# Query transposes of a linear-attention and GEGLU block: 32x32 block transposes on VectorE in place of TensorE transposes, another order of tokens, and a new order of all work

## The chip, the core and the metric

The kernel runs on one core of a Trainium2 chip. A core has four compute engines that are used here: TensorE (PE, matmuls; its weight loads are listed apart as PEld), VectorE (DVE), ScalarE (ACT) and GpSimd (POOL). A fifth, SyncE (SP), issues all transfers (DMA) between DRAM and the on-chip memory. Matmul results arrive in PSUM, in eight banks of 128 x 512 f32. The metric is the device time of one execution in microseconds (us).

## The reference

The input x has 2048 tokens of 512 channels. With xn the layer norm of x, there are 32 heads of 16 channels:

```python
q, k, v = split(xn @ wqkv)                    # 32 heads x 16
phi = lambda t: where(t > 0, t + 1, exp(t)) + 1e-6
pq, pk = phi(q), phi(k)
kv  = sum over tokens of pk (outer) v         # 16 x 16 per head
z   = sum over tokens of pk
o   = (pq @ kv) / (pq . z + 1e-6)
s   = o.reshape(S, D) @ wo
g   = silu((gelu(x @ w_gate) * (x @ w_up)) @ w_down)    # inner width 1792
out = x + s * g
```

Nothing in it depends on the order of the tokens: keys are summed over all of them, and everything else is done token by token.

## The kernel before

**Precision and products.** Everything is f32. A matmul operand is split into a high part (a cast to the reduced format fp32r) and a low part (the rest), and a product is the sum of three: high by high, low by high, high by low. The helper `sum3` issues them; its matmuls all stand on line 537, 128x128 by 128x512 each. Large products are done in 2x2 blocks with seven block products instead of eight. X, Y, Z and V are the PSUM banks of such a scheme: FX, FY, FZ in the up and gate products of the FFN, DX, DY, DZ in its down product, SX, SY, SZ in the last stage. The sums and differences that the scheme needs are VectorE and GpSimd additions.

**Stages.** First come layer norm, key and query projections, `phi` and the accumulation of keys against tokens (up to about 140 us). The scaled-up queries `qp` go to DRAM (`q_d`), with tokens on the 128 partitions. Then the FFN runs over the second 1024 tokens (p = 1, to about 345 us) and over the first 1024 (p = 0, to about 547 us), 14 steps each, with the weights stored in DRAM in split form between the two. The results `acc` get their silu and are kept, for p = 1 in DRAM (`g1_d`). The last stage multiplies the scaled queries, channels on the partitions, with a 512x512 matrix m (kv times wo, in split form `ms`), multiplies by the gate, adds x and stores the output with channels as rows.

**The queries.** Between the steps of the second FFN half stands `queries(i)`, eight calls, for two tiles of 128 tokens each. The table `PAIRS` says at which step. One call loads two tiles q (256 KB each) from DRAM; GpSimd multiplies them with the key sum (tile u, helper `tt` on line 521); VectorE reduces u over each head (line 1193), adds the small constant (1194), takes the reciprocal (1196) and scales q with it (1199). TensorE then transposes the two tiles with eight 128x128 transposes into two PSUM banks `ptq` (line 1206; the banks come from places 5, 6, 7), and ScalarE copies them into the tile pT (helper on line 515). One store of 512 KB takes pT to `pn_d`, laid out by partition, channel block and token; each piece of it is 256 tokens, 1 KB. At the start of the last stage, `s_forms` loads `pn_d` into tiles pb, 256 KB at a time; their casts and sums are the operands Xh, Xl, sf of the SX, SY, SZ products. `s_quad` then takes the gate v, the product and the row of x through its chain of VectorE and GpSimd operations.

**Memory.** Tiles live in numbered places of the pool `dp`. The queries use places 12 (q), 13 (u) and 14 (pT), one after the other; other stages use the same places before and after. `tile_in` gives a place to a new tile, and the class `Gen` remembers the tile before it, all of whose uses have to be over first.

**The order of the work.** The kernel first records every operation with an assumed duration (class `Plan`, method `do`). TensorE's order is given by a list of keys (`pe_keys`), in which ("QT", i) stands for the transposes of call i. ScalarE, VectorE, GpSimd and the transfers are ordered by a list scheduler with due times, which simulates the engines. From its first order it goes on by a table of random seeds (`STEPS`, then `MORE`): each seed moves the due times of the operations in a small window of time a little and plans again. The four engines then get their instructions in that order. All transfers are in one SyncE queue, in the order in which they become due; an entry in that queue waits until its sources are ready and its target is free, and the entries behind it wait too. There are never more than eight transfers under way: the queue waits for the one that is eight back.

The last lines of a call, as the program has them:

```python
pts = [bank(ring("ptq", [5, 6, 7]), f"ptq{t0 + n}", (P, KT, P)) for n in range(2)]
for n in range(2):
    copy("ACT", pTs[:, :, n * P:(n + 1) * P], pts[n], D, "pqT")
dma(pn_d[...](j // 2, ...), pTs, 512, "pieces")
PAIRS = {2: [0], 3: [1], 4: [2], 5: [], 6: [], 7: [3], 8: [4], 9: [5], 10: [], 11: [6], 12: [7]}
```

Of the kernel before, what the change touches and what calls it, by code (L numbers as in the profile page):

```python
# [47 lines left out]
class Gen:  # L48


    def __init__(self, prev):
        self.prev, self.ops, self.over = prev, set(), False
        if prev:
            prev.over = True

# [24 lines left out]
class Plan:  # L80
# [9 lines left out]
    MARGIN = (0.2, 0.2, 3.0)  # L90
    STEPS = (12, 17, 30, 37, 54, 58, 64, 68, 88, 91, 95, 112, 120, 130, 135, 178, 219, 243, 254, 272, 291, 296, 307, 334, 350, 358, 391, 399, 421, 482, 518, 595, 713, 745, 884, 952, 1037, 1318, 1332, 1383, 1390, 1412, 1459, 1532, 1540, 1563, 1676, 1910, 1984, 2062, 2080, 2109, 2148, 2154, 2161, 2184, 2185, 2285, 2316, 2343, 2539, 2627, 2682, 2732, 2736, 2755, 2779, 2791, 2797, 2850, 2885, 3006, 3525, 3544, 3782, 3810, 3819, 4355, 4555, 4804, 4809, 5047, 5174, 5351)
    MORE = ()
    WAIT = 0.3
# [7 lines left out]
    def do(self, eng, cost, fn, out, *ins, more=(), key=None, name="", kb=0, kind="load"):  # L101
# [32 lines left out]
        for v in (out, *more, *ins):  # L134
            if isinstance(v, View) and v.gen:
                assert not v.gen.over, name
                if v.gen.prev:
                    op.pre.update(v.gen.prev.ops)
                v.gen.ops.add(op)
# [267 lines left out]
def kernel(  # L407
# [34 lines left out]
    def tile_in(pool_name, unit, shape, dtype, name, parts=1):  # L442

        gen = gens[pool_name, unit] = Gen(gens.get((pool_name, unit)))
        kept = []
# [5 lines left out]
        return View([Res() for _ in range(parts)], get, gen, pool_name == "ps")  # L451

    count = {}
# [720 lines left out]

    pn_d = {p: dram_view([P, KT, 2 * NC], f"pn{p}_d", 4) for p in range(2)}
    zb = zacc
# [4 lines left out]

    def queries(i):

        t0 = [8, 10, 12, 14, 0, 2, 4, 6][i]
        q, w, pT = D2(12, f"q{t0}"), D2(13, f"u{t0}"), D2(14, f"pT{t0}")
        for n in range(2):
            t = t0 + n
            dma(half(q, n), q_d(t, slice(t * P, (t + 1) * P)), 256)
        den = little("den", f"den{t0}", [P, 2, H])
        for n in range(2):  # L1190
            tt("POOL", "mul", heads(half(w, n)), heads(half(q, n)), heads(zb), D, "u")
        for n in range(2):
            do("DVE", 0.602, lambda o, i: nc.vector.tensor_reduce(o, i, axis=AX.X, op=ALU.add), den[:, n], heads(half(w, n)), name="den").port = False
        do("DVE", 0.1, lambda o, i: nc.vector.tensor_add(o, o, i.unsqueeze(1).to_broadcast([P, 2, H])), den, den_eps, name="eps").port = True
        r = little("rr", f"rr{t0}", [P, 2, H])
        do("DVE", 0.275, lambda o, i: nc.vector.reciprocal(o, i), r, den, name="rr").port = False
        pTs = pT.map(lambda ap: ap.rearrange("p a d -> p (a d)").rearrange("p (k c) -> p k c", c=2 * P))
        for n in range(2):
            do("DVE", 0.602, lambda o, j: nc.vector.scalar_tensor_tensor(
                o, o, EPS, j.unsqueeze(2).to_broadcast([P, H, DH]), op0=ALU.add, op1=ALU.mult), heads(half(q, n)), r[:, n], name="pn")  # L1200
        pts = [bank(ring("ptq", [5, 6, 7]), f"ptq{t0 + n}", (P, KT, P)) for n in range(2)]

        def run_t(o, a, b, c, idn):
            for v, u in ((o, b), (c, a)):
                for k in range(KT):
                    nc.tensor.transpose(v[:, k, :], u[:, k * P:(k + 1) * P], idn)  # L1206
        do("PE", 0.95, lambda o, a, b, idn: run_t(o, b, a, pts[1](), idn), pts[0], half(q, 0), half(q, 1), ident, more=(pts[1],), key=("QT", i))
        for n in range(2):
            copy("ACT", pTs[:, :, n * P:(n + 1) * P], pts[n], D, "pqT")
        j = t0 % 8  # L1210
        dma(pn_d[0 if t0 < 8 else 1](j // 2, (slice(None), slice(None), slice(j * P, (j + 2) * P))), pTs, 512, "pieces")

    PAIRS = {2: [0], 3: [1], 4: [2], 5: [], 6: [], 7: [3], 8: [4], 9: [5], 10: [], 11: [6], 12: [7]}

    def ffn(p, groups):
        keys, todo = [], [list(g) for g in groups]
        qs = [2 * u + i for u in UNITS[p] for i in range(2)]
        for n, q in enumerate(qs):
# [10 lines left out]
            keys += [("F", p, q, 4), ("F", p, q, 3)]  # L1229
            if not p:  # L1230
                for i in PAIRS.get(n, []):
                    queries(i)
                    keys.append(("QT", i))
            if not is_up and len(todo) > 1 and todo[0][-1] != u and ("F", p, 2 * todo[0][-1] + 1, 3) in keys:
# [135 lines left out]
    def s_forms(p):  # L1370
        got = []
        for a in range(2):
# [5 lines left out]
            for k in range(2):  # L1378
                t = D2(ring("br", BR), f"pb{p}{a}{k}")
                for th in range(2):  # L1380
                    src = View([pn_d[p](j, ()).res[0] for j in range(2 * th, 2 * th + 2)],
                               pn_d[p](0, (slice(None), 2 * a + k, slice(th * NC, (th + 1) * NC))).get)
                    dma(half(t, th), src, 256)
                b += [half(t, 0), half(t, 1)]
# [4 lines left out]
    def cut(v, h, m):  # L1389
        w = NC // m  # L1390
        return v.part(v.res if len(v.res) < m else v.res[h:h + 1], (slice(None), slice(h * w, (h + 1) * w)))

    def s_quad(p, c, forms, g, xp):
# [12 lines left out]
        def block(dh, th, e, ps, to):  # L1406
            v, o = g[dh, c, th], xp[2 * dh + c]
            how = WAYS.get((n, dh, th), "A")
            k = 2 * dh + c
            m = 2 if last and (dh, th) == LAST else 1  # L1410
            if how == "C":
                tt("DVE", "add", e, e, ps, NC, "sc")
                tt("POOL", "mul", v, v, e, NC, "r")
                r = v
            else:
                if e is not None:
                    tt("DVE", "add", to, e, ps, NC, "sc")
                r = v if how == "B" else to
# [94 lines left out]
def laid_out(inputs, shape):  # L1513
# [8 lines left out]
    def piece(v):  # L1522
# [31 lines left out]
```

## Time and profile before

| | |
|---|---|
| median of three runs | 603.11 us (602.56 to 604.77) |
| span of the profiled execution | 600.9 us; the profile gives no other time of this execution |
| TensorE busy | 592.3 us of it, 2696 matmuls |
| VectorE, ScalarE, GpSimd busy | 471.4, 335.3, 357.4 us |
| transfers | 145.24 MB in 63210 packets |

The span runs from the first to the last instruction that the profile holds. The times of the runs are taken around a whole execution, so the median stands a little above the span. Three views are used. The page gives the busy time of each engine and the costliest groups of instructions. The chain of waits goes back from the last instruction: at each step to what released it, or to the instruction ahead of it on its engine. The list of waits says how long an engine stood for which producer (total, times, longest).

In a row of a group, `out<-in` names what is written and read, then come the shapes, the count, the busy time in us, the mean of one in ns, and the idle time of the engine just ahead of these instructions with what ended it. In a row for a single tile, three numbers give the minimum, median and maximum of one in ns, then when the first and the last began. In a timeline, a row begins with the start and the length in us.

### The profile page before, as it was taken

How to read it: one execution, taken by the hardware profiler on the slowest of the kernel's cores; microseconds unless marked ns; L12 is line 12 of the kernel's file. 1: busy time of each engine (PE TensorE's matmuls, PEld its weight loads, DVE VectorE, ACT ScalarE, POOL GpSimd, SP SyncE). 2: the span in 40 equal slices, each digit the busy share in tenths (PEclk: the TensorE clock that was granted, in tenths of full speed). 3: DMA queues.
4: the chain of work that ended last, by engine and by line, in shares of the span. 5: the costliest groups of instructions: out<-in, count | busy, mean ns of one | idle time of the engine just before them, and what ended most of it. 6: DMA issues, size and time to landing. Idle time of an engine off the chain costs nothing.

```text
span 600.9 us, 8255 instructions
## 1 busy us (share of the span) xinstructions
PE 592.3 (99%) x2696; PEld 489.5 (81%) x2696; DVE 471.4 (78%) x698; ACT 335.3 (56%) x611; POOL 357.4 (59%) x300
## 2 busy tenths in 40 slices
PE   8999999999999999999999999999999999999996
PEld 7888888888888888888888888887888888887884
DVE  6999988785788878899878956565655777699897
ACT  6777877876676653665455146364234650476841
POOL 5844654525678875977588317346216663469665
PEclk9999999999999999999999999999999999999999
DMA  8458422147858736954859997798479897999644
GB/s 283 154 176 297 159 70 89 70 176 269 301 175 327 273 127 234 357 197 157 280 176 398 347 324 241 257 300 304 171 248 340 292 307 252 307 331 332 222 192 158
DMA packets 63210, 145.24 MB, mean 242 GB/s; under 512 B 5696, under 2 KB 17216, under 8 KB 63168
## 3 DMA queue, kind: packets, MB, share of 16 engines
q1 hardware_dynamic: 63168, 144.73, 68.9%
q8 instruction: 21, 0.34, 0.2%
q14 instruction: 21, 0.17, 0.1%
HBM read 82.05 MB, written 62.65 MB: 241 GB/s over the span
## 4 chain that ended last, share of the span: by engine, by line
PE 97%; DVE 1%; DMA 0%; issue 0%; ACT 0%; POOL 0%; DVEq 0%; ACTq 0%
PE FX L537 25%; PE FZ L537 13%; PE DX L537 13%; PE gps L537 7%; PE DZ L537 6%; PE FY L537 6%; PE X L537 5%; PE SX L537 4%; PE DY L537 3%; PE Z L537 3%; PE q L537 2%; PE SZ L537 2%; PE k L537 2%; PE Y L537 1%; PE ptq L1206 1%; PE pt L713 1%
## 5 line engine op out<-in xcount | busy, mean ns | idle before, releaser
L537 PE MATMUL FX<-Xh,w 128*128 128x512 f32 x448 | 152.4, 390 | 0.0
L1114 POOL TENSOR_TENSOR h<-h,g 128x512 f32<-128x512 f32 x42 | 62.6, 1496 | 68.7 <-DVE h L521 61.1
L537 PEld LDWEIGHTS FX<-Xh,w 128*128 128x128 f32 x448 | 83.7, 188 | 17.1
L521 POOL TENSOR_TENSOR h<-h,h 128x512 f32<-128x512 f32 x56 | 83.7, 1494 | 18.5 <-DVE hf5l L521 4.5
L537 PE MATMUL FX<-Xl,w 128*128 128x512 f32 x224 | 87.3, 390 | 0.0
L537 PE MATMUL FZ<-Xh,w 128*128 128x512 f32 x224 | 78.0, 390 | 0.0
L515 ACT COPY fu<-FX 128x512 f32<-128x512 f32 x56 | 32.9, 588 | 60.2 <-PE FX L537 46.3
L537 PE MATMUL gps<-pks,xns 128*128 128x512 f32 x192 | 51.2, 391 | 0.0
L537 PEld LDWEIGHTS FX<-Xl,w 128*128 128x128 f32 x224 | 42.1, 188 | 8.7
L537 PEld LDWEIGHTS FZ<-Xh,w 128*128 128x128 f32 x224 | 41.9, 188 | 8.7
L789 POOL TENSOR_TENSOR zacc<-zacc,kp 128x512 f32<-128x512 f32 x16 | 24.8, 1549 | 35.0 <-DVE kp L778 34.8
L521 POOL TENSOR_TENSOR u<-q,zacc 128x512 f32<-128x512 f32 x16 | 22.5, 1427 | 37.1 <-issue 24.3
L537 PE MATMUL FZ<-Xl,w 128*128 128x512 f32 x112 | 43.7, 390 | 0.0
L537 PEld LDWEIGHTS gps<-pks,xns 128*128 128x128 f32 x192 | 35.9, 188 | 7.4
L1140 DVE TENSOR_TENSOR acc<-acc,DX 128x512 f32<-128x512 f32 x48 | 32.5, 683 | 9.0 <-PE DX L537 8.1
L537 PE MATMUL FY<-Xh,w 128*128 128x512 f32 x112 | 39.0, 389 | 0.0
L521 DVE TENSOR_TENSOR h<-fu,FZ 128x512 f32<-128x512 f32 x28 | 19.1, 684 | 22.9 <-PE FZ L537 15.5
L521 DVE TENSOR_TENSOR g<-fu,FZ 128x512 f32<-128x512 f32 x28 | 19.1, 684 | 21.9 <-PE FZ L537 14.1
L515 ACT COPY fe<-FX 128x512 f32<-128x512 f32 x28 | 16.5, 588 | 33.5 <-PE FX L537 30.4
L1106 ACT ACTIVATE g<-g 128x512 f32<-128x512 f32 x42 | 26.6, 633 | 12.9 <-DVE g L521 12.9
L537 PE MATMUL X<-kq,Xh 128*128 128x512 f32 x96 | 30.8, 397 | 0.0
L1140 DVE TENSOR_TENSOR acc<-acc,DZ 128x512 f32<-128x512 f32 x32 | 21.8, 682 | 9.5 <-PE DZ L537 7.8
(427 smaller groups left out, 1596.1 us busy)
## 6 DMA issues: line engine op xcount, KB each, us to landing
w_d<-w SPq DMA_DIRECT2D x36, 512.0 KB, 4.9
w<-w_d SPq DMA_DIRECT2D x36, 512.0 KB, 5.3
wd_d<-wd SPq DMA_DIRECT2D x21, 512.0 KB, 4.6
wd<-wd_d SPq DMA_DIRECT2D x21, 512.0 KB, 5.3
x<-in_first SPq DMA_DIRECT2D x16, 256.0 KB, 3.5
q_d<-qp SPq DMA_DIRECT2D x16, 256.0 KB, 2.1
q<-q_d SPq DMA_DIRECT2D x16, 256.0 KB, 4.9
pn_d<-pT SPq DMA_DIRECT2D x8, 512.0 KB, 6.2
```

The costliest lines, as they stand in the source:

```text
L515: do("ACT", act(n), lambda o, i: nc.scalar.copy(o, i), dst, src, name=name)
L521: do(eng, c, lambda o, p, q: getattr(e, f"tensor_{op}")(o, p, q), dst, a, b, name=name)
L537: nc.tensor.matmul(o, v[i], v[i + 1], start=start and part == 0 and i == 0, stop=stop and part == 1 and i == len(v) - 2, skip_group_check=on)
L713: nc.tensor.transpose(o[:, k, :], a[:, k * P:(k + 1) * P], b)
L789: do("POOL", pool(D), lambda o, i: nc.gpsimd.tensor_add(o, o, i), zacc, p0, name="zacc")
L1106: curved("gelu", do("ACT", curve(NC), lambda o, i: nc.scalar.activation(o, i, AF.Gelu_apprx_tanh), g, ps if e is None else g, name="gelu"))
L1114: do("POOL", pool(NC), lambda o, i: nc.gpsimd.tensor_mul(o, o, i), h, g, name="h")
L1140: do("DVE", dve(NC), lambda o, i: nc.vector.tensor_add(o, o, i), a, ps, name="acc")
L1206: nc.tensor.transpose(v[:, k, :], u[:, k * P:(k + 1) * P], idn)
```

## The change

The queries are done in four calls of four token tiles instead of eight of two (`TURNS` in place of `PAIRS`). Places 13 and 14 become one tile `wide` of 128 x 2048 for a call's four tiles (`across`, with a `Gen` that has two predecessors). It is used by blocks: for each of 16 blocks of 32 channels, four token tiles side by side, 32 channels each. GpSimd writes u there in runs of 32; VectorE reduces, and scales q as before, and then transposes each tile in blocks of 32x32 within the same tile `wide`, over u (new line 1236). Such a transpose turns each 32x32 block where it stands; it does not carry a block to other partitions. The stores do that: each takes 32 partitions, whose blocks go to the right rows of `pn_d`, which is now channels by tokens. Four stores of 256 KB per call, in pieces of 512 bytes, make 16 in place of 8 of 512 KB. The transposes of TensorE, their PSUM banks, ScalarE's 16 copies and the keys ("QT", i) are gone.

Within each 512 tokens the order becomes "32-token group, tile, token of the group" where it was "tile, token". The last stage keeps that order for its products, x and the output, which the host arranges ahead and behind. Only the gate is still in the old order, so it is read through a view in runs of 32 (`turned`), with the other operands viewed to match (`by_turn`).

Last, `STEPS` is empty and `MORE` holds 319 new seeds, so the planned order of all four engines and of the transfers is new throughout.

```diff
-    def __init__(self, prev):
-        self.prev, self.ops, self.over = prev, set(), False
-        if prev:
-            prev.over = True
+    def __init__(self, *before):
+        self.before, self.ops, self.over = [g for g in before if g], set(), False
+        for g in self.before:
+            g.over = True
...
-    STEPS = (12, 17, 30, 37, 54, 58, 64, 68, 88, 91, 95, 112, 120,
...
-    MORE = ()
+    STEPS = ()
+    MORE = (1110680, 9769299, 7540955, 3028877, 5915102, 9100519,
...
+    WIDE = (13, 14)
+    def across(parts, shape):
+
+        gen = Gen(*[gens.get(("dp", u)) for u in WIDE])
+        for u in WIDE:
+            gens["dp", u] = gen
+        return View([Res() for _ in range(parts)], lambda: shaped(wide(), shape), gen)
...
-    pn_d = {p: dram_view([P, KT, 2 * NC], f"pn{p}_d", 4) for p in range(2)}
+    BL = 32
+    NB = P // BL
+    pn_d = {p: dram_view([D, 2 * NC], f"pn{p}_d", 2) for p in range(2)}
...
+    def queries(p, th):
+
+        t0 = 8 * p + 4 * th
+        T4 = across(4, (P, D // BL, 4, BL))
+        for m in range(2):
+            t = t0 + 2 * m
+            q = D2(12, f"q{t}")
+            den = little("den", f"den{t}", [P, 2, H])
+            r = little("rr", f"rr{t}", [P, 2, H])
+            us = [T4.part((T4.res[2 * m + n],), (slice(None), slice(None), 2 * m + n)) for n in range(2)]
...
+            for n in range(2):
+                tt("POOL", "mul", us[n], by_block(half(q, n)), by_block(zb), D, "u")
...
+            for n in range(2):
+                do("DVE", 0.602, lambda o, i: nc.vector.transpose(o, i), us[n], half(q, n), name="turn").port = False
+        for a in range(NB):
+            dst = pn_d[p](th, slice(None)).map(lambda ap, a=a: ap.rearrange("(b i) c -> i b c", i=BL)[:, :, th * NC + a * P:][:, :, :P])
+            src = T4.map(lambda ap, a=a: ap[a * BL:(a + 1) * BL].rearrange("p b n e -> p b (n e)"))
+            dma(dst, src, 256, "pieces")
+
+    TURNS = {2: (1, 0), 4: (1, 1), 9: (0, 0), 11: (0, 1)}
...
-                    tt("DVE", "mul", cut(r, h, m), cut(v, h, m), cut(to, h, m), NC // m, "r")
+                    tt("DVE", "mul", rs[h], vs[h], ts[h], NC // m, "r")
...
-                tt("POOL" if (n, dh, th) in ON_POOL else "DVE", "add", x, x, cut(r, h, m), w, "xr")
+                tt("POOL" if (n, dh, th) in ON_POOL else "DVE", "add", by_turn(x), by_turn(x), rs[h], w, "xr")
...
-        "in_xt": x.T.reshape(d // P, P, 2, 2, -1).transpose(2, 0, 3, 1, 4),
+        "in_xt": x.T.reshape(d // P, P, 2, 2, 4, 4, -1).transpose(2, 0, 3, 1, 5, 4, 6).reshape(2, d // P, 2, P, -1),
...
-    return _np.ascontiguousarray(r.results[0]["out_y"].T).reshape(shape)
+    y = r.results[0]["out_y"].reshape(shape[-1], 2, 2, 4, 4, -1).transpose(1, 2, 4, 3, 5, 0)
+    return _np.ascontiguousarray(y).reshape(shape)
```

Three places show what this does to the order. In the rows, a name's last number is a buffer's; a line number is that of the program the row is from (the helper of line 537 stands on line 562 after the change, that of 521 on 546, that of 490 on 515).

TensorE, in the second FFN half, around the down product DZ031 (hf2 and hf3 are the FFN's inner values, wd its weights); before, with the transposes of the call for tiles 4 and 5:

```order
L537 MATMUL DZ031_5023<-hf3h_4502,wd32_4379 128x512
L537 MATMUL DZ031_5023<-hf2h_4693,wd22_4830 128x512
L1206 MATMUL ptq4_5030<-ident_174,q4_4886 128x128 x4
L1206 MATMUL ptq5_5031<-ident_174,q4_4886 128x128 x4
L537 MATMUL DZ031_5023<-hf2l_4733,wd22_4830 128x512
L537 MATMUL DZ031_5023<-hf2h_4693,wd22_4830 128x512
```

After, around the same product:

```order
L562 MATMUL DZ031_4864<-hf3h_4418,wd32_4454 128x512
L562 MATMUL DZ031_4864<-hf2h_4644,wd22_4538 128x512
L562 MATMUL DZ031_4864<-hf2l_4656,wd22_4538 128x512
L562 MATMUL DZ031_4864<-hf2h_4644,wd22_4538 128x512
L562 MATMUL FX3_4696<-Xh10_298,w32_4613 128x512 x2
L562 MATMUL FX3_4696<-Xl10_314,w32_4613 128x512
```

The eight transposes are gone from between the DZ matmuls, which now follow each other; the FFN products around them belong to other steps than before.

VectorE, where tiles 4 and 5 are scaled (u, q, den and rr are the tiles of `queries`, acc the FFN's sums, h22 and fu values of the FFN's product scheme); before:

```order
L1193 TENSOR_REDUCE den4_4955<-u4_4937 128x32
L1140 TENSOR_TENSOR acc0_3_3793<-acc0_3_3793,DX031_4900 128x512
L1194 TENSOR_TENSOR den4_4955<-den4_4955,den_eps_3521 128x64
L1196 RECIPROCAL rr4_4970<-den4_4955 128x64
L1199 SCALAR_TENSOR_TENSOR q4_4886<-q4_4886,rr4_4970 128x512
L1140 TENSOR_TENSOR acc0_5_3807<-acc0_5_3807,DX030_4844 128x512
L1140 TENSOR_TENSOR acc0_7_3814<-acc0_7_3814,DX031_4900 128x512
L521 TENSOR_TENSOR h22_3_4996<-fu3_3_4931,FZ3_4868 128x512
```

After:

```order
L1165 TENSOR_TENSOR acc0_7_3821<-acc0_7_3821,DZ031_4864 128x512
L1227 TENSOR_REDUCE den4_4885<-wide_204 128x32 x2
L1230 TENSOR_TENSOR den4_4885<-den4_4885,den_eps_3414 128x64
L1231 RECIPROCAL rr4_4899<-den4_4885 128x64
L1233 SCALAR_TENSOR_TENSOR q4_4770<-q4_4770,rr4_4899 128x512
L1236 STREAM_TRANSPOSE wide_204<-q4_4770 128x16x32
L1233 SCALAR_TENSOR_TENSOR q4_4770<-q4_4770,rr4_4899 128x512
L1236 STREAM_TRANSPOSE wide_204<-q4_4770 128x16x32
L546 TENSOR_TENSOR h22_3_4924<-fu3_3_4913,FZ3_4893 128x512
```

The two transposes stand behind the scalings, with no FFN work between, and the work on the bank FZ3 stands behind all of it.

SyncE's queue ahead of the last stage (ms and g are the matrix and the gates that this stage uses); before:

```order
L490 DMA ms12_5255<-m12_d_170 128x1024
L490 DMA pn0_d_84<-pT6_5213 512x1x256
L490 DMA ms11_5270<-m11_d_169 128x512
L490 DMA ms13_5291<-m13_d_171 128x1024
L490 DMA pb110_5308<-pn1_d_85 128x512 x2
L490 DMA pb111_5347<-pn1_d_85 128x512 x2
```

After:

```order
L515 DMA pn0_d_84<-wide_204 32x16x128
L515 DMA ms11_5138<-m11_d_169 128x512
L515 DMA ms13_5159<-m13_d_171 128x1024
L515 DMA pn0_d_84<-wide_204 32x16x128
L515 DMA pb111_5202<-pn1_d_85 128x512 x2
L515 DMA wide_204<-pn1_d_85 128x512 x4
```

The last store stands behind the loads of ms, and the first tiles of the last stage are loaded into `wide` behind it.

More of the change, by code (lines that the diff above doesn't have):

```diff
@@ L136, in do @@
                 assert not v.gen.over, name
-                if v.gen.prev:
-                    op.pre.update(v.gen.prev.ops)
+                for g in v.gen.before:
+                    op.pre.update(g.ops)
                 v.gen.ops.add(op)
@@ L444, in tile_in @@
         gen = gens[pool_name, unit] = Gen(gens.get((pool_name, unit)))
+        if pool_name == "dp" and unit in WIDE:
+            assert dtype == F32
+            at = WIDE.index(unit) * 2 * D
+            return View([Res() for _ in range(parts)], lambda: shaped(wide()[:, at:at + 2 * D], shape), gen)
         kept = []
@@ L1180, in heads @@
         return v.map(lambda ap: ap.rearrange(heads_ap, d=DH))
[L1182 to L1211, printed above, removed]
@@ L1213, with by_block @@
-    PAIRS = {2: [0], 3: [1], 4: [2], 5: [], 6: [], 7: [3], 8: [4], 9: [5], 10: [], 11: [6], 12: [7]}
+    def by_block(v):
+        return v.map(lambda ap: ap.rearrange("p (b e) -> p b e", e=BL))
+    def queries(p, th):
[8 more added lines that the diff above has]
+            for n in range(2):
+                dma(half(q, n), q_d(t + n, slice((t + n) * P, (t + n + 1) * P)), 256)
+            for n in range(2):
+                tt("POOL", "mul", us[n], by_block(half(q, n)), by_block(zb), D, "u")
+            for n in range(2):
+                do("DVE", 0.602, lambda o, i: nc.vector.tensor_reduce(o, i, axis=AX.X, op=ALU.add),
+                   den[:, n].map(lambda ap: ap.rearrange("p (b h) -> p b h", h=BL // DH)),
+                   us[n].map(lambda ap: ap.rearrange("p b (h d) -> p b h d", d=DH)), name="den").port = False
+            do("DVE", 0.1, lambda o, i: nc.vector.tensor_add(o, o, i.unsqueeze(1).to_broadcast([P, 2, H])), den, den_eps, name="eps").port = True
+            do("DVE", 0.275, lambda o, i: nc.vector.reciprocal(o, i), r, den, name="rr").port = False
+            for n in range(2):
+                do("DVE", 0.602, lambda o, j: nc.vector.scalar_tensor_tensor(
+                    o, o, EPS, j.unsqueeze(2).to_broadcast([P, H, DH]), op0=ALU.add, op1=ALU.mult), heads(half(q, n)), r[:, n], name="pn")
+            for n in range(2):
+                do("DVE", 0.602, lambda o, i: nc.vector.transpose(o, i), us[n], half(q, n), name="turn").port = False
[3 more added lines that the diff above has]
+            dma(dst, src, 256, "pieces")
@@ L1229, in ffn @@
             keys += [("F", p, q, 4), ("F", p, q, 3)]
[L1230 to L1233, printed above, removed]
+            if not p and n in TURNS:
+                queries(*TURNS[n])
             if not is_up and len(todo) > 1 and todo[0][-1] != u and ("F", p, 2 * todo[0][-1] + 1, 3) in keys:
@@ L1380, in s_forms @@
                 for th in range(2):
-                    src = View([pn_d[p](j, ()).res[0] for j in range(2 * th, 2 * th + 2)],
-                               pn_d[p](0, (slice(None), 2 * a + k, slice(th * NC, (th + 1) * NC))).get)
-                    dma(half(t, th), src, 256)
+                    dma(half(t, th), pn_d[p](th, (slice((2 * a + k) * P, (2 * a + k + 1) * P), slice(th * NC, (th + 1) * NC))), 256)
                 b += [half(t, 0), half(t, 1)]
@@ L1410, in block @@
             m = 2 if last and (dh, th) == LAST else 1
+            vs = [turned(v)[:, h * NB // m:(h + 1) * NB // m] for h in range(m)]
             if how == "C":
                 tt("DVE", "add", e, e, ps, NC, "sc")
-                tt("POOL", "mul", v, v, e, NC, "r")
-                r = v
+                tt("POOL", "mul", vs[0], vs[0], by_turn(e), NC, "r")
+                rs = vs
             else:
@@ L1417, in block @@
                     tt("DVE", "add", to, e, ps, NC, "sc")
-                r = v if how == "B" else to
+                ts = [by_turn(cut(to, h, m)) for h in range(m)]
+                rs = vs if how == "B" else ts
                 for h in range(m):
-                    tt("DVE", "mul", cut(r, h, m), cut(v, h, m), cut(to, h, m), NC // m, "r")
+                    tt("DVE", "mul", rs[h], vs[h], ts[h], NC // m, "r")
             for h in range(m):
```

16 lines of the change are left out of this document (15 added, 1 removed).

## The prediction

> **What bounds the kernel now.** I read the page first, for which engine is full and what the chain of waits is made of.
>
> ```profile
> span 600.9 us, 8255 instructions
> PE 592.3 (99%) x2696; PEld 489.5 (81%) x2696; DVE 471.4 (78%) x698; ACT 335.3 (56%) x611; POOL 357.4 (59%) x300
> PEclk9999999999999999999999999999999999999999
> q1 hardware_dynamic: 63168, 144.73, 68.9%
> PE 97%; DVE 1%; DMA 0%; issue 0%; ACT 0%; POOL 0%; DVEq 0%; ACTq 0%
> ```
>
> TensorE is busy for 99% of the span at an undiminished clock, and 97% of the chain is its own work. The other engines, and the DMA queues with 68.9% of their time, have slack on the average. So a microsecond counts if TensorE issues it, or if something makes TensorE wait. The second view therefore is what TensorE waits for today:
>
> ```profile
> PE warm L559 <- DVE ones L548: 1.1, 1, 1.1
> PE k L537 <- DVE Xl L521: 0.9, 1, 0.9
> PE SX L537 <- ACT su L515: 0.7, 1, 0.7
> PE pt L713 <- DVE xn L691: 0.3, 1, 0.3
> PE DZ L537 <- DVE acc L1140: 0.2, 1, 0.2
> ```
>
> These are all: 3.2 us, one wait each. The first two and the fourth lie in the first 20 us, SX in the last 10. Between them TensorE waits once, for 0.2 us. Next I looked at the chain of waits around the steps that go, in order of time (start, length, piece):
>
> ```profile
> 360.21 0.46 PE FX L537 x2
> 360.67 0.87 PE ptq L1206 x8
> 361.54 0.23 PE DY L537
> 361.77 0.92 PE FX L537 x4
> ...
> 484.78 1.36 PE FY L537 x6
> ...
> 529.01 0.87 PE ptq L1206 x8
> 529.89 1.15 PE FX L537 x5
> ```
>
> The eight transposes of one call stand without a gap between matmuls: 360.67 + 0.87 = 361.54. A full matmul takes 1.36/6 = 0.227 us of the chain (its own record is longer, since matmuls overlap), a transpose 0.87/8 = 0.109.
>
> **The change: what goes.** The query transposes leave TensorE. The eight calls stand in the chain with 0.87 us each, of which the first and the last are shown: 64 x 0.109 = **-6.97 us**. The number of full matmuls stays, 2696 - 64 = 2632 being all that is left. What they share with others goes too:
>
> ```profile
> L1206 PE MATMUL ptq<-ident,q 128*128 128x128 f32 x64 | 8.3, 272 | 0.0
> L515 ACT COPY pT<-ptq 128x512 f32<-128x512 f32 x16 | 8.7, 590 | 16.8 <-PE ptq L1206 16.8
> ```
>
> x64 confirms the count. The 16 copies out of PSUM free ScalarE of 8.7 us; it is 56% busy and on no chain here, so I put 0 on that.
>
> **What comes on VectorE.** Sixteen block transposes. The trace has none. Bounds come from VectorE's nearest rows:
>
> ```profile
> L1193 DVE TENSOR_REDUCE den<-u 128x32 f32<-128x512 f32 x16 | 10.6, 680 | 3.9 <-POOL u L521 3.9
> L682 DVE BATCH_NORM_STATS2 st<-x 128x6 f32<-128x512 f32 x16 | 10.9, 683 | 2.6 <-DMA x<-in_first 2.6
> L1199 DVE SCALAR_TENSOR_TENSOR q<-q,rr x16: 683/688/1667, 346.1 to 526.5; 128x512 f32<-128x512 f32 x16
> 596.11 0.42 DVE L521 TENSOR_TENSOR xp0l<-xp0l,SX 128x256 f32<-128x256 f32 x1
> ```
>
> Whatever passes 512 f32 elements a lane takes 0.68; 256 elements take 0.42, the lower bound; the worst instance of the row that feeds a turn (the third, minimum/median/maximum) is 1.67, the upper. I take 0.68, since a turn too passes 512 elements a lane: 16 x 0.68 = 10.9 us, between 6.7 and 26.7. Where do they land? By the windows (length, then busy us of PE, PEld, DVE, ACT and POOL, clock, DMA share, GB/s):
>
> ```profile
> 345.00:520.00 175.00, 175.00 (x809) 144.33 (x808) 109.03 (x163) 74.18 (x133) 78.73 (x62) 1.00 0.80 274
> 520.00:580.00 60.00, 59.84 (x267) 49.04 (x266) 55.69 (x78) 41.59 (x74) 46.88 (x31) 1.00 0.82 287
> 580.00:601.00 21.00, 14.88 (x70) 11.92 (x69) 16.64 (x28) 4.05 (x7) 9.36 (x8) 0.96 0.46 175
> ```
>
> All turns lie in the first window or just before it: the changed order has the last call's ahead of the last stage. There VectorE has 175 - 109 = 66 us idle, so even 26.7 us fit: **0 us** by throughput. If that cover were gone they would cost their full 10.9. The reduction, reciprocal and scaling stay as they are. GpSimd still makes 16 products u, now written in runs of 32 elements; its one strided row against a contiguous one (w1tmp, whose operand is read in runs of 128, and wd0tmp) bounds this:
>
> ```profile
> L521 POOL TENSOR_TENSOR w1tmp<-raw x2: 731/737/743, 111.3 to 119.8; 128x256 f32<-128x256 f32 x2
> L521 POOL TENSOR_TENSOR wd0tmp<-draw x2: 732/928/1124, 136.2 to 139.9; 128x256 f32<-128x256 f32 x2
> ```
>
> The minimum is the same, so 0. Twice the price would add 16 x 1.3 = 21 us to an engine with 175 - 79 = 96 idle: still 0.
>
> **The transfers.** Eight stores of 512 KB from 128 partitions become sixteen of 256 KB, each from 32 partitions in pieces of 512 bytes. The bytes stay, the pieces go from 4096 of 1 KB to 8192.
>
> ```profile
> pn_d<-pT SPq DMA_DIRECT2D x8, 512.0 KB, 6.2
> DMA to landing us min/median/max: 4.7/6.2/8.4
> pb<-pn_d SPq DMA_DIRECT2D x16, 256.0 KB, 4.2
> L490 SPq DMA_DIRECT2D pn_d<-pT x8: 518/520/599, 362.8 to 534.5; - x8
> ```
>
> The second line is the landing of those eight stores. The trace has no store from fewer than 128 partitions. For the landing of a new one I take 6.2 us, that of the nearest row (half the bytes, and as many pieces, 512). Bounds: 4.2, the 256 KB load, and 12.4, twice the median, as if a quarter of the partitions halved the pace. The queue that issues them pays 8 x 0.52 = 4.2 us more in 200 us.
>
> In a sentence of its own: the Trainium skill, page "SBUF — State Buffer", section "Door 1: The DMA port swizzle (why [64,N] ≈ [32,N])", says that the bandwidth follows the number of the 16 memory ports that the partitions reach, and that 32 adjacent partitions reach 8. This speaks against the change, and no row here shows it. By it the transfer would run at half pace; if all of the landing doubled with it, the sum would be the 607.5 of the second rival.
>
> Who would notice? One store's landing is waited for at three places; I counted the matmuls that stand between in the changed order (0.227 us each):
>
> ```profile
> L521 POOL TENSOR_TENSOR u<-q,zacc x16: 1287/1295/1767, 339.8 to 519.7; 128x512 f32<-128x512 f32 x16
> L1196 DVE RECIPROCAL rr<-den x8: 546/553/554, 345.5 to 522.8; 128x64 f32<-128x64 f32 x8
> L1106 ACT ACTIVATE g<-g 128x512 f32<-128x512 f32 x42 | 26.6, 633 | 12.9 <-DVE g L521 12.9
> L515 ACT COPY fu<-FX 128x512 f32<-128x512 f32 x56 | 32.9, 588 | 60.2 <-PE FX L537 46.3
> ```
>
> - **A and B**, between the two calls of one half. The fused tile is filled again, so GpSimd's first u of the second call waits for all four stores. Behind u stand, on VectorE, two reductions, the small addition, the reciprocal, two scalings and two turns, and then the work that frees the FFN's banks. In B the last store is 75 matmuls (17.0 us) ahead of the product FZ3 that needs such a bank. Behind the landing come u 1.3, and on VectorE 2 x 0.68 + 0.1 + 0.55 + 4 x 0.69 + the bank's own 0.68 = 5.5; with 1.6 for the store's issue and some ten hand-overs (an estimate: 0.5 and 0.1 each) 8.4. Left for the landing: 17.0 - 8.4 = **8.6 us**. A has 63 matmuls, 14.3 us, to a product FX; behind the landing come u 1.3, a reduction 0.68, the addition that makes a gate 0.68, its gelu 0.63, a copy on ScalarE 0.59, and by the same estimate 1.6 for issue and hand-overs, 5.5 in all: 8.8 us.
> - **C**, the start of the last stage. The reload waits for all stores. Today's chain there is in the timelines:
>
> ```profile
> 534.46 0.52 SPq L490 DMA_DIRECT2D pn_d<-pT  x1
> 540.76 0.80 SPq L490 DMA_DIRECT2D pb<-pn_d  x2
> 547.37 1.09 PE L537 MATMUL SX<-Xh,ms 128*128 128x512 f32 x4
> ```
>
> From the store's issue to the first SX now takes 547.37 - 534.46 = 12.9 us, in which the store lands after 6.3. In the changed order the last store stands 67 matmuls before the SX that needs the cast, 15.2 us. Left for the landing: 6.3 + 15.2 - 12.9 = **8.6 us**.
>
> All three forgive 8.6 us; the slowest of today's stores needed 8.4. At 6.2 I put **0**; at 12.4, 3 x (12.4 - 8.6) = +11.4.
>
> **New order of tokens.** In the last stage 14 VectorE products read one operand in runs of 32 elements instead of 512; two products and seven additions on GpSimd too. Only GpSimd's w1tmp row shows a strided operand, at no extra; VectorE's scaling row reads one operand with each element repeated 16 times, at the usual 0.688. I take 0. Twice the price is a rival below.
>
> **New order of all work.** The seeds move the planner's list everywhere. TensorE's waits sum to 3.2 us now, so a better order can win at most that, with nothing gained from the transposes' place; a worse one may open waits of its own. The head and the last products stand as before in the changed order: 0, bounds -3.2 and as many new ones, +3.2.
>
> **Sum.** 600.9 - 6.97 + 0 = 593.9 us of span. The median of the runs shown, 603.1, is 2.2 above the profiled span; with it, **596.1 us**, 1.2% less.
>
> **The rivals.**
>
> - **Some waits come back.** For: a planner that places work by assumed durations leaves three margins of 2 us or so, and landings vary by 3.7 us among eight stores; VectorE had one place, DZ, where it was already late. Against: the present order had the same kind of margin at C and lost nothing. At 10 us of landing, 3 x 1.4 = 4.2: 600.3. From 598 to 602.
> - **Slower: the stores from 32 partitions are late.** Place: A, B and C alike. Price: landing less 8.6 at each. It decides over the gain from 8.6 + 7.0/3 = 10.9 us on; at 12.4 the sum is 596.1 + 11.4 = 607.5, and at 14 it is 612.3. For: nothing here shows 32 partitions, and DMA engines are 80% busy in that window. Against: the pieces of the new stores are the same in number as of one old store, with half the bytes. In a sentence of its own: by the skill's rule the chance would be higher, but only the transfer's own time doubles by it, not the waiting ahead of it.
> - **Strided operands double VectorE's 14 products.** That adds 14 x 0.68 = 9.5 us, nearly all in 520 to 580, where 4.3 are idle: +5.2, and about 0.5 at the end: 601.8, no difference to be told. Against: the scaling row.
> - **The new order also takes up the old waits.** 596.1 - 3.2 = 592.9. Against: at the head and at the end the changed order has the same instructions ahead of the same products.
> - **That the change does nothing:** if the transposes ran in TensorE's idle time. The gapless chain excludes it.
>
> **How the numbers follow.** The sum 0.68 (594.6 to 598), some waits 0.13, late stores 0.07, strided operands 0.06, old waits taken 0.06. A difference of 0.5%, 3.0 us, is about what a measurement of this kernel can tell: faster means under 600.1, slower over 606.1. Faster: 0.68 + 0.06 + half of the second case, 0.07 = 0.81. Slower: 0.07. The same: 0.12. The range is 593.5 to 600.6: it takes the first case, half of the last and most of the second, and leaves out late stores and strided operands.
>
> **What would show it.** TensorE with 2632 matmuls and about 585 us busy, no ptq or pT row; a transpose row of VectorE, 16 times at about 0.68, and VectorE at 482 us; ScalarE at 326. Four thousand more packets, and a row of sixteen 256 KB stores that land in 8 us or less. TensorE's waits as now, with none over 1 us before FX, FZ or the first SX. The prediction is wrong if that store row reads over 9 us and such waits appear, if a turn takes much over 1 us and VectorE holds the FFN's banks, or if VectorE's last-stage products read over 0.8 us.

## The result, and the profile after

The changed kernel takes 597.46 us (median of four runs, 596.48 to 598.76) against 603.37 us for the kernel before (also of four runs; the 603.11 of the table is the median of the first three). The ratio is 0.990, with a 95% interval of 0.988 to 0.992. The forecast was 596.1 us, in a range of 593.5 to 600.6, so the time came out as forecast, 1.4 us above the sum. The page of the changed kernel, in the lines that answer to those of before:

```profile
span 595.2 us, 8108 instructions
PE 585.9 (98%) x2632; PEld 482.0 (81%) x2632; DVE 490.1 (82%) x714; ACT 326.1 (55%) x595; POOL 356.5 (60%) x300
DMA packets 67434, 145.24 MB, mean 244 GB/s; under 512 B 5824, under 2 KB 21440, under 8 KB 67392
PE 90%; DVE 5%; DMA 2%; issue 1%; ACT 0%; SPq 0%; DVEq 0%; ACTq 0%
```

TensorE has 64 instructions less and is still nearly always busy; 4224 packets more are there for the same bytes. The profiled span fell by 5.7 us, not by the 6.97 of the sum. The chain no longer is TensorE almost alone: between 538 and 574 us, around the start of the last stage, it goes through VectorE for several stretches and through one load of 5.0 us. The new instructions, by tile and by transfer (in the first row minimum, median and maximum in ns; in the second, us to landing):

```profile
L1236 DVE STREAM_TRANSPOSE wide<-q x16: 667/711/711, 339.2 to 520.2; 128x512 f32<-128x512 f32 x16
pn_d<-wide SPq DMA_DIRECT2D x16, 256.0 KB, 5.8
```

A turn takes 0.71 us and a store lands after 5.8. Next, what TensorE waits for, and the one new wait of GpSimd that the prediction spoke of (places A and B):

```profile
PE warm L584 <- DVE ones L573: 1.1, 1, 1.1
PE DX L562 <- DVE acc L1165: 1.0, 1, 1.0
PE k L562 <- DVE Xl L546: 0.9, 1, 0.9
PE SX L562 <- ACT su L540: 0.7, 1, 0.7
PE SX L562 <- DVE xp L546: 0.2, 1, 0.2
```
```profile
POOL wide L546 <- DMA pn_d<-wide: 5.5, 2, 3.4
```

GpSimd does wait twice for stores to land, 5.5 us in all. No FX or FZ product of TensorE waits for that. TensorE's own waits sum to 3.9 us, 0.7 more than before. The new one of 1.0 us is a down product, and its place is just ahead of the last stage:

```profile
539.13 1.74 POOL L546 TENSOR_TENSOR h<-h,h 128x512 f32<-128x512 f32 x1
541.45 1.73 POOL L546 TENSOR_TENSOR pb<-wide,pb 128x512 f32<-128x512 f32 x1 [0.57 <-DMA wide<-pn_d]
```
```profile
539.64 0.68 DVE L1165 TENSOR_TENSOR acc<-acc,DZ 128x512 f32<-128x512 f32 x1
540.24 1.18 DVE L546 TENSOR_TENSOR hf0l<-h,hf0h 128x512 fp32r<-128x512 f32 x1
541.35 0.68 DVE L546 TENSOR_TENSOR Xl<-pb,Xh 128x512 fp32r<-128x512 f32 x1
541.95 1.78 DVE L546 TENSOR_TENSOR hf0l<-h,hf0h 128x512 fp32r<-128x512 f32 x1
543.65 1.27 DVE L1165 TENSOR_TENSOR acc<-acc,DX 128x512 f32<-128x512 f32 x2
```
```profile
544.38 0.50 PE L562 MATMUL DX<-hf1h,wd 128*128 128x512 f32 x1 [1.05 <-DVE acc L1165]
```

GpSimd starts at 541.45 as soon as the reloaded queries have landed, and ends at 543.18. VectorE's subtraction hf0l starts inside that time and takes 1.78 us in place of 0.68: it finishes 0.55 after GpSimd does. The sum acc behind it is what frees TensorE's bank.

### The profile page after: what moved, and what is told of

It reads as the page before. It is cut to its first block, busy times and chain, and to the rows that moved or that the text cites. A ratio compares the mean times of both kernels' runs of the same rounds, so it can differ in the third digit from the quotient of the medians.

```text
span 595.2 us, 8108 instructions
## 1 busy us (share of the span) xinstructions
PE 585.9 (98%) x2632; PEld 482.0 (81%) x2632; DVE 490.1 (82%) x714; ACT 326.1 (55%) x595; POOL 356.5 (60%) x300
## 4 chain that ended last, share of the span: by engine, by line
PE 90%; DVE 5%; DMA 2%; issue 1%; ACT 0%; SPq 0%; DVEq 0%; ACTq 0%
PE FX L562 24%; PE FZ L562 12%; PE DX L562 12%; PE gps L562 7%; PE FY L562 6%; PE X L562 6%; PE DZ L562 5%; PE DY L562 3%; PE Z L562 3%; PE SX L562 2%; PE k L562 2%; PE q L562 2%; PE Y L562 1%; PE SZ L562 1%; PE pt L738 1%
## 5 line engine op out<-in xcount | busy, mean ns | idle before, releaser
L562 PE MATMUL FX<-Xh,w 128*128 128x512 f32 x448 | 150.7, 389 | 0.0
L1139 POOL TENSOR_TENSOR h<-h,g 128x512 f32<-128x512 f32 x42 | 63.9, 1522 | 85.4 <-DVE h L546 71.2
L546 POOL TENSOR_TENSOR wide<-wide 128x256 f32<-128x256 f32 (+1 forms) x38 | 40.2, 1066 | 18.1 <-DVE m L546 4.7
L546 POOL TENSOR_TENSOR wide<-q,zacc 128x512 f32<-128x512 f32 x16 | 21.0, 1334 | 16.6 <-DMA q<-q_d 6.6
```

The lines of the kernel that those rows point to most:

```text
L546: do(eng, c, lambda o, p, q: getattr(e, f"tensor_{op}")(o, p, q), dst, a, b, name=name)
L562: nc.tensor.matmul(o, v[i], v[i + 1], start=start and part == 0 and i == 0, stop=stop and part == 1 and i == len(v) - 2, skip_group_check=on)
L1139: do("POOL", pool(NC), lambda o, i: nc.gpsimd.tensor_mul(o, o, i), h, g, name="h")
```

## The experiments

Two theories stood against each other. The first is that of the prediction: TensorE is full, so 7 us less of its work are 7 us less of time, and the rest is covered. The second: the new order of all work is what counts. Times are medians beside runs of the kernel before on the same chip, with the ratio to these and its interval.

**The transposes left out, in the old order.** ScalarE's copies take q as it is.

```diff
-            for v, u in ((o, b), (c, a)):
-                for k in range(KT):
-                    nc.tensor.transpose(v[:, k, :], u[:, k * P:(k + 1) * P], idn)
+            return
...
```

> The kernel before with the 64 TensorE transposes left out and all else in the old order (ScalarE's 16 copies stay and take q untransposed, so the queries of the last stage are not transposed; a few loads move by a place in SyncE's queue). Theory 1, the gain is TensorE's own time: the eight gaps that the transposes leave in the row of matmuls add up to 7.2 us in the trace of before, so 603.4 - 7.2 = 596.2 us, 595.5 to 597. Theory 2, the gain comes from the new order of all work: 600 us or more, with new waits of TensorE where the transposes stood. If theory 1 holds and this is faster than the changed kernel (597.5), the new order costs about 1.3 us.

Measured: 601.56 us, ratio 0.997 (0.996 to 0.998). Only 1.9 us of the 7.2 came. What TensorE waits for in this run:

```profile
PE FZ L537 <- DVE g L521: 1.6, 1, 1.6
...
PE DX L537 <- DMA wd<-wd_d: 0.5, 1, 0.5
PE DY L537 <- ACT hf0h L515: 0.5, 1, 0.5
...
```

Four engines and the transfers had been set to meet a TensorE that spends 0.9 us on each call. Without that, it comes to seven products between 405 and 546 us before their operands or banks are there, by 0.3 to 1.6 us. These waits sum to 4.1 of the 5.3 us that it gives back. Theory 1 fails in its plain form: a full TensorE is no proof that the others keep up with a faster one.

**The same, with all work planned anew.** The transposes count 0 in the plan, and 35 seeds found for it replace the old ones.

```diff
-        do("PE", 0.95, lambda o, a, b, idn: run_t(...
+        do("PE", 0.0, lambda o, a, b, idn: run_t(...
-    STEPS = (12, 17, 30, 37, 54, 58, 64, 68, 88, 91, 95, 112, 120,
+    STEPS = ()
+    MORE = (7922960, 3719368, 3670536, 7710866, 4767403, 729595,
...
```

> The kernel before with its TensorE transposes left out (as in the first run of that kind, queries not transposed), and now all work planned anew: the transposes count nothing in the plan, and 35 seeds of its own take the place of the old ones. New theory, the removal is worth its 7.2 us only when the other engines' order makes room for a TensorE that is 7 us earlier: 603.4 - 7.2 = 596.2, 595 to 597.5, with TensorE's waits in the second FFN half gone. Rival, the old supply of weights and operands cannot go faster in any order: 599 to 602, as before re-planning (601.6).

Measured: 595.17 us, ratio 0.987 (0.985 to 0.988), span 594.2. TensorE's waits:

```profile
PE warm L559 <- DVE ones L548: 1.1, 1, 1.1
PE SX L537 <- ACT su L515: 0.7, 1, 0.7
PE pt L713 <- DVE xn L691: 0.5, 1, 0.5
PE k L537 <- ACT Xh L515: 0.3, 1, 0.3
```

All waits between the head and the last product are gone, and the time is 7.9 us below before. So the removal is worth what the chain said, under the condition that the order follows. This run also has none of the change's other parts; the changed kernel is 2.3 us above it (1.5 in its version with a few more seeds, measured beside it). That is what the turns, the fused tile and the small stores cost together in the orders that were found; the searches were not equally long (35 seeds here, 322 there).

**Order alone.** Two runs with TensorE's transposes in place: the old seeds left out, and 12 more behind them.

```diff
-    STEPS = (12, 17, 30, 37, 54, 58, 64, 68, 88, 91, 95, 112, 120,
...
+    STEPS = ()
```

> The kernel before with its table of seeds emptied: the planner's first order of all work, nothing moved by seeds. Theory, both kernels' times hang on a searched order: TensorE gets new waits of 2 to 8 us, 605 to 612 us. Rival, the order matters little while TensorE is full: 603 to 605.

Measured: 603.76 us, ratio 1.000 (0.999 to 1.002). The rival holds: in the kernel before, the seeds are worth nothing that can be measured.

```diff
-    MORE = ()
+    MORE = (8831671, 6995616, 91112, 6691839, 7169725, 9334311,
...
```

> The kernel before, transposes in place, with 12 more seeds after its own: as good a new order as a longer search found. Theory, TensorE waits for 3.2 us in all, most of it at the head and the end, so an order alone wins 0 to 1.5 us: 602 to 603.4. Rival, the changed kernel's gain could have been had by order alone: 600 or less.

Measured: 603.17 us, ratio 1.000 (0.999 to 1.001). Order alone did not bring the gain. Twelve seeds are a short search, and a long one was not run; but the waits that an order could remove there sum to 3.2 us, less than the 5.9 us gained.

**The changed kernel without its seeds.**

```diff
-    MORE = (1110680, 9769299, 7540955, 3028877, 5915102, 9100519,
...
+    MORE = ()
```

> The changed kernel with its 319 new seeds left out: block transposes, tile `wide`, stores and order of tokens as changed, in the planner's first order. Theory, the transposes' place is worth 7 us only in an order that was searched for it: TensorE waits take up the 7 us and more, so no faster than the kernel before, 603 to 615. Rival, the gain is the removal and the seeds only polish it: 597 to 600, and 7 us less than the kernel before without seeds.

Measured: 610.97 us, ratio 1.013 (1.012 to 1.015). Everything that the change does, in the planner's first order, is 7.5 us slower than the kernel before beside it (603.50), and the seeds are worth 13.5 us. (The table of the changed kernel holds 322 seeds; the number 319 given above and in the expectations is wrong.) Two of TensorE's new waits, one of GpSimd's, and what VectorE did during the first:

```profile
PE DZ L562 <- DVE hf6l L546: 3.7, 1, 3.7
PE SX L562 <- ACT Xh L540: 1.4, 1, 1.4
```
```profile
POOL pb L546 <- DMA wide<-pn_d: 7.7, 1, 7.7
```
```profile
332.07 1.27 DVE L1227 TENSOR_REDUCE den<-wide 128x32 f32<-128x512 f32 x2
...
334.21 1.29 DVE L1233 SCALAR_TENSOR_TENSOR q<-q,rr 128x512 f32<-128x512 f32 x2
335.43 1.30 DVE L1236 STREAM_TRANSPOSE wide<-q 128x512 f32<-128x512 f32 x2
336.65 1.25 DVE L546 TENSOR_TENSOR hf6l<-h,hf6h 128x512 fp32r<-128x512 f32 x2
```

The work for a pair of query tiles is a block of 4.6 us on VectorE, of which 1.2 are turns. Here it stands ahead of hf6l, and TensorE waits. The wait costs more than its 3.7 us, since TensorE's clock is lower behind it. The page of this run has the granted clock in 40 slices of the span, in tenths of the full clock; an 8 stands in mid-span:

```profile
PEclk9999999999999999999999899999999999999998
```

From 338.0 to 341.6 us the granted clock is 0.55, and the ten matmuls behind the wait take 3.98 us where ten at 0.227 take 2.27: 1.7 us more. Most of the rest of the loss lies in the last stage: TensorE there waits for casts and differences of reloaded queries, and GpSimd waits 7.7 us for the reload.

**The turns left out, and done twice.** Both in the changed kernel's planned order.

```diff
-                do("DVE", 0.602, lambda o, i: nc.vector.transpose(o, i), us[n], half(q, n), name="turn").port = False
+                do("DVE", 0.602, lambda o, i: None, us[n], half(q, n), name="turn").port = False
```

> The changed kernel with the 16 block transposes left out and the planned order kept (the stores carry the products u instead of the turned queries, so the last stage reads wrong values; they can start 0.7 us earlier; a few loads move by a place in SyncE's queue). Theory 1, the turns are covered as planned: 597 to 597.7, no change. Theory 2, since the same turns done twice cost 5.7 us for 11.2 us of VectorE, each costs about half of its time in any order: 597.5 - 5.6 = 592 or so, below the 595.2 of the kernel with neither kind of transpose. In between, 595.5 to 597: only the wait at 543 us goes.

Measured: 597.00 us, ratio 0.990 (0.987 to 0.992), VectorE 480.1 us busy in place of 490.1. Ten microseconds of VectorE cost nothing where the new order put them. The wait for acc of 1.0 us is still there, so the turns did not cause it.

```diff
-                do("DVE", 0.602, lambda o, i: nc.vector.transpose(o, i), us[n], half(q, n), name="turn").port = False
+                do("DVE", 0.602, lambda o, i: [nc.vector.transpose(o, i), nc.vector.transpose(o, i)], us[n], half(q, n), name="turn").port = False
```

> The changed kernel with each of the 16 block transposes done twice, the second time over the first with the same result: 16 x 0.70 = 11.2 us more of VectorE, all between 338 and 522 us. Theory: VectorE's turns are covered by its idle time there (50 us in 345 to 520 after the change), so 597.5 to 598.5. Rival: the turns stand ahead of work that TensorE waits for (two per pair, 1.4 us), so each of the eight pairs can cost up to 1.4: up to 608.

Measured: 603.19 us, ratio 1.000 (0.999 to 1.001): 11 us more of VectorE cost 5.7, nearly the whole gain. They came back as many small waits. The list of TensorE's waits now sums to 6.9 us in place of 3.9, so it holds 3.0 of the 6.4 us by which the span grew; the rest is in shorter gaps. The wait for acc grew from 1.0 to 1.3 us. The largest of the new ones are these:

```profile
PE FZ L562 <- DVE g L546: 0.8, 1, 0.8
...
PE FZ L562 <- DVE h L546: 0.7, 1, 0.7
PE DX L562 <- DVE hf6l L546: 0.6, 1, 0.6
```

The changed kernel's window in which most turns lie (length, then busy us of PE, PEld, DVE, ACT and POOL):

```profile
345.00:520.00 175.00, 175.00 (x782) 144.10 (x781) 124.80 (x182) 70.06 (x123) 83.60 (x66) 1.00 0.84 289
```

VectorE has 50 us idle there, so its throughput did not forbid it. Its queue is in order, and a pair of turns more stands ahead of the values g and h that free the FFN's banks. The wait of 0.8 us for g, on VectorE and then on TensorE:

```profile
352.85 2.79 DVE L1236 STREAM_TRANSPOSE wide<-q 128x512 f32<-128x512 f32 x4
355.56 0.65 DVE L546 TENSOR_TENSOR g<-fu,FZ 128x512 f32<-128x512 f32 x1
```
```profile
356.27 0.73 PE L562 MATMUL FZ<-Xh,w 128*128 128x512 f32 x2 [0.79 <-DVE g L546]
```

**The turns done twice, with the plan told so.** The cost in the plan is doubled, and 38 seeds were searched on from the changed kernel's last state.

> The changed kernel with each block transpose done twice, as in the first run of that kind (603.2 us), but with the doubled time known to the plan: the changed order is planned anew from its last state with 38 further seeds. Theory, VectorE has the room (50 us idle in 345 to 520), and what the unplanned doubling cost was bursts ahead of work that TensorE waits for: 598 to 600.5. Rival, VectorE's time counts there in any order: 603 again.

Measured: 610.97 us, ratio 1.013 (1.010 to 1.015), worse than without re-planning. Neither theory gave this. One place explains about half of the 13.5 us above the changed kernel. TensorE's wait, the chain that ends in it (start, length, piece), and GpSimd's wait:

```profile
PE FZ L566 <- DVE h L550: 4.0, 1, 4.0
```
```profile
388.05 5.75 DMA q<-q_d
...
393.87 1.30 POOL wide L550
...
395.19 0.69 DVE den L1231
...
402.49 0.58 DVE h L550
```
```profile
POOL wide L550 <- DMA q<-q_d: 13.6, 1, 13.6
```

The load of q left SyncE's queue at 388.05, when GpSimd had been waiting for it for 7.8 us (its 13.6 us end at 393.87); VectorE then stood for u, and after it the whole block of 7.3 us, four turns in it, ran ahead of h, for which TensorE waited 4.0 us. Here too the clock is lower behind the wait (the 7 in mid-span):

```profile
PEclk9999999999999999999999999979999999999998
```

From 403.2 to 409.0 us it is 0.50, and fourteen matmuls take 6.08 us where fourteen at 0.227 take 3.18: 2.9 us more, so this place costs about 6.9. Whether a good order for doubled turns exists stays open: this run shows only that the plan is trusted too far where it takes a load's landing for granted ahead of such a block.

**The stores.** First, from 128 partitions with the same bytes and pieces.

```diff
-            dst = pn_d[p](th, slice(None)).map(lambda ap, a=a: ap.rearrange("(b i) c -> i b c", i=BL)[:, :, th * NC + a * P:][:, :, :P])
-            src = T4.map(lambda ap, a=a: ap[a * BL:(a + 1) * BL].rearrange("p b n e -> p b (n e)"))
+            dst = pn_d[p](th, slice(None)).map(lambda ap, a=a: ap[a * P:(a + 1) * P, th * NC:(th + 1) * NC].rearrange("p (b c) -> p b c", c=P))
+            src = T4.map(lambda ap, a=a: ap.rearrange("p b n e -> p b (n e)")[:, a::NB])
```

> The changed kernel with the 16 stores taken from 128 partitions instead of 32: as many bytes, pieces of 512 bytes and issues, but each store takes four of the 16 blocks of all partitions, and the DRAM side is written in 2 KB rows, so that the blocks don't arrive at their places (the last stage reads queries in a wrong arrangement). Theory: the landing time, 5.8 us median from 32 partitions, is mostly queueing behind other transfers, so it falls by less than 1.5 us, and the time stays: 597 to 598. Rival, 32 partitions halve the pace: landing falls to about 3 to 4 us, GpSimd's waits for the stores (5.5 us) go, and if TensorE's wait at 543 us came from a late reload, up to 1 us is won: 596.5.

Measured: 597.50 us, ratio 0.990 (0.989 to 0.992).

```profile
pn_d<-wide SPq DMA_DIRECT2D x16, 256.0 KB, 5.5
```

5.5 us from 128 partitions against 5.8 from 32. In the other runs of the changed kernel with its 32 partitions the same row reads between 5.2 and 6.0. So 32 partitions cost nothing that shows here. The Trainium skill, page "SBUF — State Buffer", section "Door 1: The DMA port swizzle (why [64,N] ≈ [32,N])", has half the pace from half the ports, about 218 GB/s from 8 and 436 from 16. By these figures, as an estimate, 256 KB take 1.2 us in place of 0.6. A difference of 0.6 us is less than the 0.8 by which the row varies between runs, so this run neither shows the rule nor speaks against it; what it excludes is that the whole landing doubles.

Second, each store issued twice, first to a spare place.

```diff
+    again_d = dram.tile([P, D // BL, P], F32, name="again_d")
...
-            dma(dst, src, 256, "pieces")
+            do("SP", 0.475, lambda o, i, a=a: [nc.sync.dma_start(again_d[a * BL:(a + 1) * BL], i), nc.sync.dma_start(o, i)], dst, src, kb=256, kind="pieces", name="pieces")
```

> The changed kernel with each of the 16 stores issued twice, first to a spare place in DRAM and then to its own, so 4 MB more and a later landing, with the order of the engines kept. Theory, the three places forgive a landing of 8.6 us: if the last store of a call lands within that of its old place, GpSimd waits longer than the 5.5 us it does now, and TensorE by less than 1 us more: 597 to 599. Rival, no slack is left at the last stage: each us of lateness shows, 600 or more.

Measured: 600.68 us, ratio 0.996 (0.994 to 0.997): 3.2 us more, so the rival is nearer.

```profile
L1241 SPq DMA_DIRECT2D pn_d<-wide x16: 318/416/673, 353.7 to 538.6; - x16
```
```profile
PE pkv L1314 <- DMA wide<-g_d: 1.3, 2, 1.1
PE DX L562 <- DMA again_d<-wide: 0.9, 1, 0.9
```

The median landing stayed at 5.9 us. But the last store left at 538.6 us in place of 531.6: the queue has eight transfers under way at most, so this store left when the transfer eight back had landed, and what stands behind the stores in the queue is late. So this is mainly the price of more transfers in one queue, which the places A, B and C did not count, rather than of a slower landing; their 8.6 us were not put to the test by it, and the two effects were not told apart further.

**One instruction moved.** The sum acc goes ahead of the subtraction hf0l that GpSimd stretched.

```diff
-    for o in plan.order(pe_keys):
+    work = plan.order(pe_keys)
+    at = {o.n: i for i, o in enumerate(work)}
+    late = work.pop(at[2745])
...
+    work.insert(at[2790], late)
+    for o in work:
         o.fn()
```

> The changed kernel with one VectorE instruction moved: the sum acc3 (operand DX in PSUM), which TensorE waits for 1.05 us at 543 us, goes ahead of the subtraction hf0l that stood before it and that took 1.78 us in place of 0.68 while GpSimd ran. Theory: the loss at the last stage is this one collision, so the wait of 1.0 us goes and the time falls to 596.6, with the span at 594.2 to 594.5. Rival: the work of the last stage is simply late, since the reloaded queries arrive late, and the wait moves to the next product: no change, 597.5.

Measured: 596.87 us, ratio 0.989 (0.987 to 0.991).

```profile
PE DX L562 <- DVE acc L1165: 0.5, 1, 0.5
```
```profile
541.86 1.82 DVE L546 TENSOR_TENSOR Xl<-pb,Xh 128x512 fp32r<-128x512 f32 x1
543.60 0.67 DVE L1165 TENSOR_TENSOR acc<-acc,DX 128x512 f32<-128x512 f32 x1
544.20 0.68 DVE L546 TENSOR_TENSOR hf0l<-h,hf0h 128x512 fp32r<-128x512 f32 x1
```

The wait halved, but GpSimd's operation, from 541.84 to 543.14, now met the instruction ahead, Xl, which took 1.82 us. The collision moved, and hf0l behind it is short again. The time is not told apart from the changed kernel's.

**A few seeds more.** Four behind the 322; the numbers in the expectation, seven and 319, are wrong.

> The changed kernel with 7 more seeds behind its 319. Theory, what is left to win by order is the waits of about 1.3 us that the changed order added: 596 to 597.5. Rival: the chip doesn't follow the plan to less than 1 us, so it may as well be slower, 597.5 to 599.

Measured: 596.68 us, ratio 0.989 (0.987 to 0.991). Not told apart from the changed kernel either. No version that was tried and does all of the work beats it beyond the intervals.

## Why the prediction was right, and where it was not

- **The transposes, -6.97 us: right.** The eight gaps between the starts of the matmuls around them measure about 7.2 us beyond the usual 0.227 a matmul, and leaving them out in a suited order gave 7.9 in the median.
- **The order, 0: the step that failed.** The prediction took the new order for a side matter, with bounds of 3.2 us, and reasoned that a full TensorE with few waits just gets shorter. In the old order the removal gave 1.9 us, and the change in the planner's first order was 7.5 us slower than before. The seeds are worth 13.5 us in the changed kernel and nothing in the one before, so the loss without them lies far outside the bound of 3.2. The number came out since the order on record was a searched one; the prediction had not asked how good it was, and in this it was lucky. The bound should have come from how late the FFN's operands and banks arrive once TensorE is 0.9 us faster per call, not from today's waits.
- **VectorE's turns, 0.68 each and covered: right as planned, for a narrower reason.** They measure 0.71 (estimated 0.68), and leaving them out changes nothing. The cover was taken from 66 us of idle time in the window. Done twice, they cost 5.7 us although the 50 us idle in that window were far more than the 11 added: what covers them is their place in the queue, not the sum.
- **VectorE at 482 us: 490.** The 16 turns are 11.0 of the 18.7 us more. Part of the rest is instructions stretched beside GpSimd, as hf0l in the rows above: all 14 of its kind take 16.7 us in place of 13.1.
- **The stores, 6.2 us and no stall: right.** 5.8 us. GpSimd waited 5.5 us at A and B, and TensorE not at all.
- **C, the last stage: 0 was too good.** The first SX did not wait. But the reload, once there, started GpSimd on top of VectorE's work, and this is the wait of 1.0 us, which fell to 0.5 when the sum was moved ahead of hf0l.
- **The sum.** TensorE's last matmul starts 5.52 us earlier (595.33 before, 589.81 after), where the transposes made about 7.2. Of the 1.7 us between, the list of waits holds 0.7; the rest lies in short gaps, and their causes stay open. The median then is 597.46 - 595.2 = 2.3 us above the profiled span, close to the assumed 2.2. Of these, 1.8 lie between the profiled execution's own time, 596.98, and its span; the rest is that it was one of the faster ones.
- **Rivals.** "Some waits come back" describes the outcome best, at 1.4 us instead of 2 to 6. Late stores from 32 partitions: no, they landed after 5.8 us. Strided operands: no, the last stage's products read as before:

```profile
L546 DVE TENSOR_TENSOR SX<-g,SX 128x512 f32<-128x512 f32 x2 | 1.4, 681 | 0.0
L546 DVE TENSOR_TENSOR SZ<-acc,SZ 128x512 f32<-128x512 f32 x1 | 0.7, 689 | 0.0
```

These are products with the gate (g, acc) read in runs of 32: 0.68 and 0.69 us, where the kernel before has 0.696 and 0.695 in the same two rows.

## What to carry to other kernels

Where one engine is full and a planner has fitted the others to it, time taken off that engine may become a full gain only after the others are planned anew (here 1.9 us before and 7.9 after): leave the work out once in the old order and once in a new one, and the difference is the price of the order. Idle time of an engine in a window covers new work only if that work does not stand in its queue ahead of something the full engine waits for; look for the longest unbroken block, not for the sum.

## What the runs showed of the hardware

- VectorE's 32x32 block transpose of 128x512 f32 takes 0.71 us, about as long as an elementwise operation of that size (0.68).
- In these rows, an operation of VectorE with both operands outside PSUM that begins while GpSimd runs is done only after it: hf0l took 1.78 and 1.18 us and ended some 0.55 after GpSimd each time. An Xl that began 0.10 us ahead of GpSimd took its 0.68; in the run with one instruction moved, one that began 0.02 us behind GpSimd's start took 1.82. The sum acc, with one operand in PSUM, ran in 0.68 inside GpSimd's 539.13 to 540.87. The Trainium skill, page "SBUF — State Buffer", section "Terms", has a port pair for which the two engines contend and which one of them locks for a whole instruction, and these rows agree with it.
- In this loaded queue, a store of 256 KB landed about as fast from 32 partitions as from 128 (5.8 and 5.5 us).
- TensorE's clock was halved for a few us behind a long wait: behind 3.7 us the granted clock was 0.55 and behind 4.0 us it was 0.50, with a matmul every 0.43 us in place of 0.227, which added 1.7 and 2.9 us. In the other runs, in which no wait in the list exceeds 1.6 us, the clock shows no such stretch in mid-span.
